# The first block of a fused attention and expert kernel: four head pairs or two halves

## Chip, cores and metric

The kernel runs on one core of a Trainium2 chip. The metric is the time of one execution in microseconds (us), measured on the device. The kernel before takes 502.85 us, the median of 6 runs (502.19 to 503.13).

The engines are named as in the profile: PE is TensorE (matmuls), PEld its weight loads, DVE is VectorE, ACT is ScalarE, POOL is GpSimd, SP is SyncE.

## What is computed

The inputs q, k and v have 8 batches, 8 heads, 1024 positions and 64 dimensions per head. E and F project the 1024 positions of the keys and values to 64. Attention over these 64 projected positions feeds a feed-forward layer with a gated activation.

```python
def _attn_ref(q, k, v, E, F):
    k_proj = np.einsum('ks,bhsd->bhkd', E, k)
    v_proj = np.einsum('ks,bhsd->bhkd', F, v)
    scores = (1.0 / np.sqrt(q.shape[-1])) * np.matmul(q, k_proj.transpose(0, 1, 3, 2))
    scores = scores - np.max(scores, axis=-1, keepdims=True)
    attn = np.exp(scores)
    attn = attn / (np.sum(attn, axis=-1, keepdims=True) + 1e-09)
    return np.matmul(attn, v_proj)

def _moe_ref(x, w_in, w_out):          # x: 8192 x 512, w_in: 512 x 2048, w_out: 2048 x 512
    h = x @ w_in
    g = h * np.clip(h + 3.0, 0.0, 6.0) / 6.0
    return g @ w_out
```

## The kernel before, in words

**Stages.** Every batch of 1024 tokens is worked on as two blocks of 512. For each block the feed-forward layer forms `g` in 16 groups of 128 columns (`fo`), each group from four matmul pairs over `ko` (`first_group`, `h_part`; the matmul itself is line 169, in `in_columns`), and then four groups of output rows (`second_group`). Attention for the next batch is slipped in between these groups at places that the program writes out by hand. The order on each engine is the order in which the Python code issues instructions (`manual_schedule`), so the position of a call in the code is its position in the engine's queue.

**Batch 0.** It has nothing to hide behind. The class `First` handles it, and `first_block` does attention for its first 512 tokens. The heads go in four pairs, `j` = 0 to 3. For each pair:

- `keys(j)` (line 375) projects k by E in 8 matmuls of 128 columns; two DVE copies (line 378) bring the result to `kp`, once for each half of the partitions.
- `queries(0, (j,))` (line 405) transposes q in 4 PE transposes; a DVE copy (line 409) brings it to SBUF.
- `keys_transposed(j)` (line 384) transposes the two heads of `kp`; a DVE copy (line 386) makes `kT`.
- `scores(j)` (line 418) forms the scores in 4 matmuls of 64x64 weights on the four quarters of the array; two exponentials on ACT follow (line 445).
- `sums(j)` (line 425 with `ones` as weights) sums the exponentials on PE; ACT takes the inverse by a logarithm and an exponential (lines 450 and 451).
- `vals(j)` (line 391) projects v by F in 8 matmuls of 128 columns; a copy (line 394) makes `vp`.
- `products(j)` (line 425 with `vp` as weights, then a multiply on DVE, line 454) writes `xT`, the input of the feed-forward layer.

The pairs overlap: `keys` of pair j is issued ahead of `scores` of pair j-1 and `sums` of pair j-2. `meanwhile` puts the first matmul pair of the feed-forward layer (group 0, `ko` 0) into the end of the block. After `first_block` come `ko` 1 and 2 of group 0, `ko` 0, 1, 2 of group 1, `ko` 3 of both, and then the groups from `fo` = 2 on without a break.

**Dummies.** `busy(n)` (line 89) issues n matmuls of 128x512 whose result nobody reads. Twelve of them stand first in PE's queue; their weights are `ones`, which DVE fills at the very start. `ident` is the identity for the PE transposes. POOL makes it (`make_identity`) after its first two DMA issues. E and F are cast by DVE and ACT (lines 140 and 141), transposed by 8 PE transposes (line 145), and copied to `e_t` (line 147, DVE) and `f_t` (line 149, ACT).

**Loads.** POOL issues all loads of q, k, v, `w_in` and `w_out`, which convert to bf16 on the way. For batch 0 the order is k and q by pairs, then v by pairs, then `w_in` in eight pieces, q's second half, `w_out`. Eight semaphores take turns on these DMAs, so each issue waits until the eighth one before it has landed.

**PSUM.** Two pools of four buffers each rotate: `pmm()` (tag mm) and `pat()` (tag at). A tile that is taken waits for the readers of the tile that had its buffer before.

**Batch 1.** `turn` (line 212) turns the projected keys by a transposing DMA on SP; `q_transposed` (line 157) does the same for q in two DMAs, heads 0 to 3 (pairs 0 and 1) and heads 4 to 7 (pairs 2 and 3). `Attention.visit(0)` then issues the scores of three pairs (line 229) with their exponentials (line 238):

```python
js = 2, 0, 1
tiles = [self.scores(j, *two) for j, two in zip(js, ((pmm, pmm), (pat, pat), (pat, pat)))]
```

`visit(1)` starts with the sums and values of pair 0 and the scores of pair 3; `visit(2)` with the sums and values of pair 1.

Of the kernel before, what the change touches and what calls it, by code (L numbers as in the profile page):

```python
# [9 lines left out]
bf16 = mybir.dt.bfloat16  # L10
# [5 lines left out]
def kernel(  # L16
# [11 lines left out]
    nc = tc.nc  # L28
    B, H, S, D = q.shape
    KP = E.shape[0]  # L30
# [3 lines left out]
    P = 128  # L34
    SO = S // P
    KO = d_model // P
    FO = d_ff // P
    TOK = 512
# [42 lines left out]
    ones = consts.tile([P, TOK], bf16, name="ones")  # L81
    nc.vector.memset(ones, 1.0)  # L82
    ident = consts.tile([P, P], bf16, name="ident")


    def busy(n):
        ps = pmm()
        for _ in range(n):
            nc.tensor.matmul(ps, ones[:, :P], ones, start=True, stop=True)  # L89

    busy(12)

    def raw_tile(name):
        return kqv_pool.tile([P, H, SO, D], bf16, tag=name, name=name)


    kqv = {0: {n: raw_tile(n) for n in ("k", "q", "v")}}
    q0 = kqv[0]["q"].rearrange("p h s d -> p (h s d)").rearrange(
        "p (t h s d) -> p t h s d", t=NB, h=H, s=SB)

    def load_q0(t, hs):
        nc.gpsimd.dma_start(out=q0[:, t, hs], in_=kqv_dram["q"][0][:, hs, t * SB:(t + 1) * SB, :])  # L102

    def load_pair(n, j):
        hs = slice(2 * j, 2 * j + 2)
        nc.gpsimd.dma_start(out=kqv[0][n][:, hs], in_=kqv_dram[n][0][:, hs])  # L106

    for j in range(KO):
        load_pair("k", j)
        load_q0(0, slice(2 * j, 2 * j + 2))  # L110
        if j == 0:
            make_identity(nc, ident)
    for j in range(KO):
        load_pair("v", j)

    def load_kqv(b, order="qkv"):
        kqv[b] = {}
# [19 lines left out]
    e_t = consts.tile([P, SO, KP], bf16, name="e_t")  # L137
    f_t = consts.tile([P, SO, 2, KP], bf16, name="f_t")
# [48 lines left out]
    class Attention:  # L187
# [143 lines left out]

        def visit(self, n):
            if n == 0:
                js = 2, 0, 1
                tiles = [self.scores(j, *two) for j, two in zip(js, ((pmm, pmm), (pat, pat), (pat, pat)))]
                for j, two in zip(js, tiles):
                    self.exps(j, two)
                return lambda: None
            if n == 1:
                den, av = self.sums(0, pmm, pmm), self.values(0, pat, pat)  # L340
                last = self.scores(3, pat, pat)
                rec = rec_tile()
# [21 lines left out]
    class First:  # L364
# [4 lines left out]
            self.vp = att.tile([P, H, D], bf16, tag="vp", name="vp")  # L369
            self.qT, self.aT = {}, {}  # L370

        def keys(self, j):
            ps = pat()[:KP, :P]
            for so in range(SO):
                nc.tensor.matmul(ps, e_t[:, so, :], kqv[0]["k"][:, 2 * j:2 * j + 2, so, :],
                                 start=(so == 0), stop=(so == SO - 1))
            for a in range(2):
                nc.vector.tensor_copy(self.kp[:, 2 * j:2 * j + 2, a, :],
                                      ps.rearrange("p (h d) -> p h d", d=D))

        def keys_transposed(self, j):
            ps = pat().bitcast(bf16)[:, :P]
            for a in range(2):
                nc.tensor.transpose(ps[:, a * KP:(a + 1) * KP],
                                    self.kp[:, 2 * j + a].rearrange("p a d -> p (a d)"), ident[:KP, :KP])
            nc.vector.tensor_copy(self.kT[:, 2 * j:2 * j + 2, :].rearrange("p h m -> p (h m)"), ps)

        def vals(self, j, copy):
            ps = pat()[:, :P]
            for so in range(SO):  # L390
                nc.tensor.matmul(ps, f_t[:, so].rearrange("p a m -> p (a m)"),
                                 kqv[0]["v"][:, 2 * j:2 * j + 2, so, :],
                                 start=(so == 0), stop=(so == SO - 1))
            copy(self.vp[:, 2 * j:2 * j + 2, :].rearrange("p h d -> p (h d)"), ps)

        def queries(self, t, js):

            ps = pat().bitcast(bf16)[:, :len(js) * TOK]
            for i, j in enumerate(js):
                for a in range(2):  # L400
                    for m in range(2):
                        o = i * TOK + a * HT + m * P
                        n = width if t else P
                        for lo in range(0, P, n):
                            nc.tensor.transpose(ps[lo:lo + n, o:o + P],  # L405
                                                q0[:, t, 2 * j + a, 2 * m:2 * m + 2, :].rearrange(
                                                    "p s d -> p (s d)")[:, lo:lo + n], ident)
            q = rec_tile().rearrange("p i n -> p (i n)").bitcast(bf16)[:, :2 * TOK]
            nc.vector.tensor_copy(q[:, :len(js) * TOK], ps)
# [24 lines left out]
            return self.quads(lambda r, h: self.vp[r:r + KP, h, :], t, j, alloc)  # L434


        def first_block(self, meanwhile):
            recs = {}

            def scores(j):  # L440
                aT = att.tile([P, 2, HT], bf16, tag="aT0", name="aT0", bufs=KO)
                tiles = [pmm() for _ in range(2)]
                self.scores(0, j, tiles, 0)
                for r in range(2):
                    nc.scalar.activation(aT[:, r], tiles[r][:, :HT], AF.Exp, scale=scale)
                self.aT[0, j] = aT

            def sums(j):
                recs[j] = opool.tile([P, TOK], f32, tag="o_sb", name="o_sb")
                nc.scalar.activation(recs[j], self.sums(0, j, pmm), AF.Ln)  # L450
                nc.scalar.activation(recs[j], recs[j], AF.Exp, scale=-1.0)

            def products(j):
                nc.vector.tensor_mul(self.xT[:, j, 0, :], self.values(0, j, pat), recs[j])

            for j in range(KO):
                self.keys(j)
                if j > 1:
                    sums(j - 2)
                self.queries(0, (j,))  # L460
                if j > 0:
                    scores(j - 1)
                else:
                    busy(1)
                self.keys_transposed(j)
                if j < 2:
                    busy(1)
            scores(KO - 1)
            self.vals(0, nc.vector.tensor_copy)
            sums(KO - 2)  # L470
            self.vals(1, nc.vector.tensor_copy)
            products(0)
            sums(KO - 1)
            self.vals(2, nc.vector.tensor_copy)
            products(1)
            busy(1)
            products(2)
            self.vals(3, nc.scalar.copy)
            meanwhile()
            products(3)  # L480

# [102 lines left out]
    def meanwhile():  # L584
        early.append(TwoGroups(xT, 0, g[0]))
        early[0].part(0, (0,))
# [48 lines left out]
    for b in range(1, B):  # L635
# [36 lines left out]
        for t in range(NB):  # L672
            g = g_tile()
            for fo in range(FO):
# [13 lines left out]
                n = t * SB + slots.index(fo)  # L688
# [43 lines left out]
```

## Time and profile before

| | before |
|---|---|
| median of 6 runs | 502.85 us (502.19 to 503.13) |
| the profiled execution | 502.73 us |
| its span (first to last instruction) | 500.9 us |
| PE busy | 494.2 us (99% of the span) |
| DVE busy | 285.3 us (57%) |
| ACT busy | 239.5 us (48%) |
| POOL busy | 38.6 us (8%) |

In the views, times count from the start of the span. In a row of the timeline the two figures are start and length, then engine, line, operation, tiles (written from read), shape and count; what stands in brackets is how long the engine was idle before and what ended that. A length of several instructions runs from the first start to the last end, and a matmul's end is modelled, so consecutive matmuls overlap in these rows. A busy share near 100% of PE does not mean that PE runs at its full rate.

### The profile page before, as it was taken

Reading aid. Unit: us, or ns where it says so; the run is one execution under the profiler, and the core shown is the slowest. Engines: PE = TensorE matmul, PEld = TensorE weight load, DVE = VectorE, ACT = ScalarE, POOL = GpSimd, SP = SyncE. Lnnn points to the kernel's source line nnn. Section 1 sums busy time; section 2 is a strip of 40 time slices with the busy share of each in tenths; the row PEclk is TensorE's granted clock in tenths of the full one; section 3 lists DMA queues with packets and bytes.
Section 4 is the critical chain, followed back from the end, with each engine's and each line's share of the span. In section 5 each row is a group of like instructions: output and inputs, shape, how many; then the busy total and the mean of one; then the engine's idle time right before and its main releaser. Section 6 shows DMA issues by size and latency. Waiting matters only on the chain.

```text
span 500.9 us, 11177 instructions
## 1 busy us (share of the span) xinstructions
PE 494.2 (99%) x4802; PEld 256.3 (51%) x4802; DVE 285.3 (57%) x438; ACT 239.5 (48%) x414; POOL 38.6 (8%) x58
## 2 busy tenths in 40 slices
PE   8899999999999999999999999999999999999997
PEld 4454544555555545555555555555455555555554
DVE  3581835976659675666648655674755656334420
ACT  3656566665355345433564344643456344343431
POOL 8620020200020020002000020000000000000000
PEclk9999999999999999999999999999999999999999
DMA  9999999897759699549950799309411261101112
GB/s 165 198 204 208 186 175 232 151 208 171 184 95 223 158 205 215 111 117 226 210 114 22 176 192 222 78 24 232 116 43 44 56 180 44 43 22 43 44 43 84
DMA packets 83618, 68.43 MB, mean 137 GB/s; under 512 B 38256, under 2 KB 69232, under 8 KB 83568
## 3 DMA queue, kind: packets, MB, share of 16 engines
q0 software_dynamic: 32480, 29.36, 37.5%
q1 hardware_dynamic: 50864, 38.02, 30.5%
q8 instruction: 37, 0.61, 0.5%
q10 hardware_dynamic: 224, 0.33, 0.3%
q14 instruction: 13, 0.11, 0.1%
HBM read 71.83 MB, written 16.97 MB: 177 GB/s over the span
## 4 chain that ended last, share of the span: by engine, by line
PE 92%; DMA 5%; POOL 2%; SPq 1%; issue 0%; ACT 0%; DVE 0%; ACTq 0%; POOLq 0%
PE mm L169 85%; DMA qT<-q 3%; PE at L169 2%; DMA v<-in_v_dram 2%; PE mm L250 1%; PE at L229 1%; PE at L250 1%; PE mm L229 1%; POOL q L102 1%; POOL k L106 1%; POOL v L106 0%; SPq L157 0%; SPq L212 0%; PE at L425 0%; PE at L405 0%
## 5 line engine op out<-in xcount | busy, mean ns | idle before, releaser
L514 DVE SCALAR_TENSOR_TENSOR g<-r,mm 128x512 bf16<-128x512 f32 x256 | 174.3, 687 | 143.6 <-ACT r L513 142.9
L169 PE MATMUL mm<-w_out_sb,g 128*64 128x512 bf16 (+2 forms) x2080 | 235.6, 376 | 0.0
L169 PE MATMUL mm<-xT,w_in_sb 128*64 128x512 bf16 x2048 | 231.1, 379 | 0.0
L513 ACT ACTIVATE r<-mm 128x512 f32<-128x512 f32 x256 | 152.7, 598 | 74.3 <-PE mm L169 73.3
L169 PEld LDWEIGHTS <-w_in_sb 128*64 128x64 bf16 x2048 | 115.8, 110 | 104.7 <-issue 0.6
L169 PEld LDWEIGHTS <-g 128*64 128x64 bf16 x2080 | 115.0, 110 | 106.3 <-issue 7.1
L548 ACT COPY o_sb<-mm 128x512 f32<-128x512 f32 x58 | 33.9, 585 | 149.8 <-PE mm L169 149.4
L270 DVE TRANSPOSE_TENSOR_REDUCE parts<-aT 128x32 f32<-128x1024 bf16 x24 | 28.8, 1226 | 0.0
L262 DVE TENSOR_TENSOR xT<-at,rec 128x512 bf16<-128x512 f32 x32 | 20.5, 683 | 8.5 <-ACT rec L181 5.8
L238 ACT ACTIVATE aT<-at 128x512 bf16<-128x512 f32 x38 | 20.7, 622 | 8.0 <-PE at L229 8.0
L262 DVE TENSOR_TENSOR xT<-mm,rec 128x512 bf16<-128x512 f32 x24 | 15.5, 686 | 7.3 <-PE mm L250 7.2
L219 POOL COPY mark<-qT 1x1 bf16<-1x1 bf16 x5 | 0.9, 177 | 202.7 <-DMA qT<-q 202.7
L205 DVE CAST kp<-at 64x512 bf16<-64x512 f32 x14 | 9.0, 678 | 11.3 <-PE at L169 11.2
L238 ACT ACTIVATE aT<-mm 128x512 bf16<-128x512 f32 x18 | 9.7, 605 | 7.5 <-PE mm L229 7.5
L169 PE MATMUL at<-k,e_t 128*64 128x512 bf16 x56 | 13.2, 379 | 0.0
L169 PE MATMUL at<-v,f_t 128*64 128x512 bf16 x56 | 13.2, 379 | 0.0
L208 DVE CAST vp<-at 64x512 bf16<-64x512 f32 x14 | 9.7, 694 | 0.4
L538 DVE COPY o_sb<-mm 128x384 f32<-128x384 f32 x1 | 0.6, 558 | 15.2 <-PE mm L169 15.2
L169 PEld LDWEIGHTS <-e_t 128*64 128x64 bf16 x56 | 6.2, 110 | 5.7
L89 PE MATMUL mm<-ones 128*128 128x512 bf16 x18 | 7.3, 540 | 1.5 <-DVE ones L82 1.5
L229 PEld LDWEIGHTS <-kT 64*64 64x64 bf16 x224 | 5.7, 106 | 5.2 <-issue 4.3
L503 DVE TENSOR_TENSOR xT<-at,rec 128x512 bf16<-128x512 f32 x4 | 2.5, 684 | 8.1 <-PE at L425 8.1
(68 smaller groups left out, 151.3 us busy)
## 6 DMA issues: line engine op xcount, KB each, us to landing
out_dram<-o_sb SPq DMA_DIRECT2D x63, 256.0 KB, 4.1
rec<-turned_rows SPq DMA_DIRECT2D x48, 256.0 KB, 6.0
k<-in_k_dram POOLq DMA_DIRECT2D x7, 1024.0 KB, 10.8
v<-in_v_dram POOLq DMA_DIRECT2D x7, 1024.0 KB, 16.0
q<-in_q_dram POOLq DMA_DIRECT2D x7, 1024.0 KB, 20.4
w_out_sb<-in_moe_w_out_dram POOLq DMA_DIRECT2D x4, 512.0 KB, 16.0
w_in_sb<-in_moe_w_in_dram POOLq DMA_DIRECT2D x5, 256.0 KB, 9.8
k<-in_k_dram POOLq DMA_DIRECT2D x4, 256.0 KB, 5.8
```

Source lines behind the costliest of these rows:

```text
L89: nc.tensor.matmul(ps, ones[:, :P], ones, start=True, stop=True)
L169: nc.tensor.matmul(ps[lo:lo + width], stationary[:, lo:lo + width], moving, **flags)
L205: nc.vector.tensor_copy(self.kp[:, :, a, :], self.ps[:KP].rearrange("p (h d) -> p h d", d=D))
L208: nc.vector.tensor_copy(self.vp[a * KP:(a + 1) * KP], self.ps[KP:].rearrange("p (h d) -> p h d", d=D))
L229: nc.tensor.matmul(tiles[r][t * KP:(t + 1) * KP, a * HT:(a + 1) * HT], self.kT[r * D:(r + 1) * D, 2 * j + a, :], qT[r * D:(r + 1) * D, j, ...
L238: when(lambda r=r: nc.scalar.activation(aT[:, :, r, :], tiles[r].rearrange("p (a n) -> p a n", a=2), AF.Exp, scale=scale))
L250: nc.tensor.matmul(tiles[t][c:c + D], stationary(r, 2 * j + a), self.weights(j, a)[r:r + KP], start=True, stop=True)
L262: when(lambda t=t: nc.vector.tensor_mul(self.xT[:, j, t, :], av[t], rec[:, t]))
L270: nc.vector.tensor_reduce(out=self.parts[:, j], op=ALU.add, axis=mybir.AxisListType.X, apply_transpose=True, in_=self.aT[j].rearrange("p a ...
L513: nc.scalar.activation(r, h_ps, AF.Relu, bias=0.5, scale=1.0 / 6.0)
L514: nc.vector.scalar_tensor_tensor(g[:, fo, :], r, 1.0, h_ps, op0=ALU.min, op1=ALU.mult)
L548: (copy or nc.scalar.copy)(o_sb, o_ps)
```

## The change

Batch 0's first block handles the heads in two halves of two pairs instead of four pairs.

- The loads of k and of q's first block come in two pieces each, those of v in three (pairs 0 and 1 together, then 2, then 3).
- `keys` projects a half in 8 matmuls of 256 columns, with two DVE copies of 64x256; `keys_transposed` does four heads and one copy of 128x256; `vals` does pairs 0 and 1 together in matmuls of 256 columns, and pairs 2 and 3 singly, with ACT copying both of these.
- The copies of queries of odd pairs go from DVE to ACT.
- Within a half, all steps of both pairs follow one another: keys, queries, transposes, scores, sums. The sums of pair 3 move into the middle of the first `vals`. `products(2)` moves behind both single `vals`.
- The dummies use `ident` as weights, so they wait for POOL to make it. The first group has 7 of them in place of 12; the block itself has others, at new places.
- Batch 1 issues its scores in the order 0, 1, 2, with the PSUM pools by position as before.

On PE there are 25 matmuls fewer: 16 of `keys`, 8 of `vals` and one dummy.

```diff
     def busy(n):
         ps = pmm()
         for _ in range(n):
-            nc.tensor.matmul(ps, ones[:, :P], ones, start=True, stop=True)
-
-    busy(12)
+            nc.tensor.matmul(ps, ident, ones, start=True, stop=True)
...
-    for j in range(KO):
-        load_pair("k", j)
-        load_q0(0, slice(2 * j, 2 * j + 2))
-        if j == 0:
+    pairs = range(KO)
+    half = KO // 2
+    for js in (pairs[:half], pairs[half:]):
+        load_pairs("k", js)
+        load_q0(0, heads(js))
+        if js[0] == 0:
             make_identity(nc, ident)
-    for j in range(KO):
-        load_pair("v", j)
+            busy(7)
+    for js in (pairs[:half], *([j] for j in pairs[half:])):
+        load_pairs("v", js)
...
             if n == 0:
-                js = 2, 0, 1
+                js = 0, 1, 2
...
-        def vals(self, j, copy):
-            ps = pat()[:, :P]
+        def vals(self, js, copy, halfway=lambda: None):
+            ps = pat()[:, :len(js) * P]
             for so in range(SO):
-                nc.tensor.matmul(ps, f_t[:, so].rearrange("p a m -> p (a m)"),
-                                 kqv[0]["v"][:, 2 * j:2 * j + 2, so, :],
+                nc.tensor.matmul(ps, f_t[:, so].rearrange("p a m -> p (a m)"), kqv[0]["v"][:, heads(js), so, :],
                                  start=(so == 0), stop=(so == SO - 1))
-            copy(self.vp[:, 2 * j:2 * j + 2, :].rearrange("p h d -> p (h d)"), ps)
-
-        def queries(self, t, js):
+                if so == SO // 2 - 1:
+                    halfway()
+            copy(self.vp[:, heads(js), :].rearrange("p h d -> p (h d)"), ps)
+
+        def queries(self, t, js, copy=nc.vector.tensor_copy):
...
-            for j in range(KO):
-                self.keys(j)
-                if j > 1:
-                    sums(j - 2)
-                self.queries(0, (j,))
-                if j > 0:
-                    scores(j - 1)
-                else:
-                    busy(1)
-                self.keys_transposed(j)
-                if j < 2:
-                    busy(1)
-            scores(KO - 1)
-            self.vals(0, nc.vector.tensor_copy)
-            sums(KO - 2)
-            self.vals(1, nc.vector.tensor_copy)
+            for js in (pairs[:half], pairs[half:]):
+                self.keys(js)
+                if js[0] == 0:
+                    busy(2)
+                for j in js:
+                    self.queries(0, (j,), nc.scalar.copy if j % 2 else nc.vector.tensor_copy)
+                self.keys_transposed(js)
+                busy(1)
+                for j in js:
+                    scores(j)
+                busy(2)
+                for j in js[:None if js[0] == 0 else -1]:
+                    sums(j)
+            self.vals(pairs[:half], nc.vector.tensor_copy, lambda: sums(KO - 1))
             products(0)
-            sums(KO - 1)
-            self.vals(2, nc.vector.tensor_copy)
             products(1)
-            busy(1)
+            self.vals((2,), nc.scalar.copy)
+            self.vals((3,), nc.scalar.copy)
             products(2)
-            self.vals(3, nc.scalar.copy)
             meanwhile()
             products(3)
```

More of the change, by code (lines that the diff above doesn't have):

```diff
@@ L99, with heads, load_pairs @@
         "p (t h s d) -> p t h s d", t=NB, h=H, s=SB)
+    def heads(js):
+        return slice(2 * js[0], 2 * js[-1] + 2)
     def load_q0(t, hs):
         nc.gpsimd.dma_start(out=q0[:, t, hs], in_=kqv_dram["q"][0][:, hs, t * SB:(t + 1) * SB, :])
-    def load_pair(n, j):
-        hs = slice(2 * j, 2 * j + 2)
+    def load_pairs(n, js):
+        hs = heads(js)
         nc.gpsimd.dma_start(out=kqv[0][n][:, hs], in_=kqv_dram[n][0][:, hs])
-    for j in range(KO):
-        load_pair("k", j)
-        load_q0(0, slice(2 * j, 2 * j + 2))
-        if j == 0:
+    pairs = range(KO)
[4 more added lines that the diff above has]
+        if js[0] == 0:
             make_identity(nc, ident)
-    for j in range(KO):
-        load_pair("v", j)
+            busy(7)
+    for js in (pairs[:half], *([j] for j in pairs[half:])):
+        load_pairs("v", js)
     def load_kqv(b, order="qkv"):
@@ L370, in __init__, with keys @@
             self.qT, self.aT = {}, {}
-        def keys(self, j):
-            ps = pat()[:KP, :P]
+        def keys(self, js):
+            ps = pat()[:KP, :len(js) * P]
             for so in range(SO):
-                nc.tensor.matmul(ps, e_t[:, so, :], kqv[0]["k"][:, 2 * j:2 * j + 2, so, :],
+                nc.tensor.matmul(ps, e_t[:, so, :], kqv[0]["k"][:, heads(js), so, :],
                                  start=(so == 0), stop=(so == SO - 1))
             for a in range(2):
-                nc.vector.tensor_copy(self.kp[:, 2 * j:2 * j + 2, a, :],
-                                      ps.rearrange("p (h d) -> p h d", d=D))
@@ L381, in keys_transposed @@
[L381 to L386, printed above, removed]
-        def vals(self, j, copy):
-            ps = pat()[:, :P]
+                nc.vector.tensor_copy(self.kp[:, heads(js), a, :], ps.rearrange("p (h d) -> p h d", d=D))
@@ new lines, in keys_transposed @@
+        def keys_transposed(self, js):
+            ps = pat().bitcast(bf16)[:, :len(js) * P]
+            for i in range(2 * len(js)):
+                nc.tensor.transpose(ps[:, i * KP:(i + 1) * KP],
+                                    self.kp[:, 2 * js[0] + i].rearrange("p a d -> p (a d)"), ident[:KP, :KP])
+            nc.vector.tensor_copy(self.kT[:, heads(js), :].rearrange("p h m -> p (h m)"), ps)
+        def vals(self, js, copy, halfway=lambda: None):
+            ps = pat()[:, :len(js) * P]
@@ L408, in queries @@
             q = rec_tile().rearrange("p i n -> p (i n)").bitcast(bf16)[:, :2 * TOK]
-            nc.vector.tensor_copy(q[:, :len(js) * TOK], ps)
+            copy(q[:, :len(js) * TOK], ps)
             for i, j in enumerate(js):
```

## Prediction

> **What bounds the kernel now.** I read the page first: its span and the busy line.
>
> ```profile
> span 500.9 us, 11177 instructions
> ...
> PE 494.2 (99%) x4802; PEld 256.3 (51%) x4802; DVE 285.3 (57%) x438; ACT 239.5 (48%) x414; POOL 38.6 (8%) x58
> ```
>
> TensorE (PE) is busy for all but 6.7 us, and no other engine for more than 57%. A change ahead of the steady stream is therefore worth what it moves the stream's start. The chain of waits for the first 36 us tells what sets that start:
>
> ```profile
> 9.79 9.75 DMA v<-in_v_dram
> ...
> 19.59 0.62 PE at L391 x8
> 20.21 0.34 PE mm L169 x2
> ...
> 20.57 0.40 PE at L425 x2
> 20.97 12.86 PE mm L169 x118
> ```
>
> Columns are start, length, what. The last quarter of v is issued at 9.79 and lands at 19.54; eight projections, a product and then 118 matmuls follow with no gap. The timeline of PE gives durations, and a second hole at batch 1's scores:
>
> ```profile
> 1.46 5.13 PE L89 MATMUL mm<-ones 128*128 128x512 bf16 x12 [1.46 <-DVE ones L82]
> ...
> 6.94 0.59 PE L89 MATMUL mm<-ones 128*128 128x512 bf16 x2
> 7.62 0.63 PE L375 MATMUL at<-k,e_t 128*64 128x128 bf16 x8
> ...
> 20.90 12.93 PE L169 MATMUL mm<-xT,w_in_sb 128*64 128x512 bf16 x118
> ...
> 66.96 1.89 PE L169 MATMUL mm<-w_out_sb,g 128*64 128x512 bf16 x16
> 69.16 0.41 PE L229 MATMUL mm<-qT,kT 64*64 64x256 bf16 x8 [0.31 <-DMA qT<-q]
> ```
>
> Twelve dummies take 5.13 us, 0.43 each; two later ones start 0.22 apart. So PE runs at half rate at first and at full rate from about 6.3, 4.8 us after its first matmul, though the granted-clock column says 1.00 in all these rows. Next, DMA by stretch (the last figure is GB/s, the third from the end the granted clock):
>
> ```profile
> 5.50:7.50 2.00, 2.00 (x13) 0.92 (x11) 0.63 (x2) 0.45 (x1) 2.00 (x3) 1.00 1.17 143
> 9.50:17.50 8.00, 7.10 (x87) 4.46 (x85) 3.81 (x14) 5.57 (x14) 5.49 (x8) 1.00 1.28 204
> ```
>
> Last, of POOL's timeline, the row that finishes `ident`:
>
> ```profile
> 3.07 0.29 POOL masks.py:199 TENSOR_SCALAR_AFFINE_SELECT ident<-ident 128x128 bf16<-128x128 bf16 x1
> ```
>
> As yardstick I take the start of column group fo=2. Before it come seven pairs from 20.90: 0.24 + 6 x 0.2155, so 22.44.
>
> **Loads.** Twelve issues of k, q, v become seven, bytes unchanged. POOL saves 5 x 0.72 us of issuing, on no path: POOL then waits for landings. The stretch 5.5 to 7.5 moved 143 GB/s against 204 later; a queue filled with larger pieces could win back 2 x 61/204 = 0.6 us. So v's last quarter lands between 18.9 and, if nothing improves, 19.54. I take 19.0; either serves, as the next part shows. Later loads (w_in and on) move with it and have slack.
>
> **The first block's chain.** What the halves do to PE's order matters more. Four short rounds, each filling the others' waits, become two long ones, in which PE stands behind its own copies. On the clock of the trace:
>
> Start. `ident` is ready at 3.36 now; two larger issues ahead of it (0.77 us for a 512 KB one against 0.72) make it 3.45. The dummies, and all that PE has queued behind them, now wait for it and start at 3.5 instead of 1.46. What hides this wait: the first real work, E and F, is cast only at 5.96. Seven dummies at 0.427 reach 6.5. If full rate comes 4.8 us after the start, as now, it comes at 8.3; then the eight transposes cost a quarter of a dummy, 0.107 each (0.06 now), their last ends at 7.55, and e_t is copied by 8.0 (0.42). The two dummies behind run until 8.3. First keys: 8.3, against 7.62.
>
> First half. Keys, 8 x 256 columns: 8 x 0.109 (half of 0.216) and the last one's way out, 1.05: 9.35. Two kp copies, 64x256, do not occur now; 64x128 takes 0.28 (starts 0.20 apart), 64x512 0.68 (0.60 apart). On the line between, 0.42 and 0.33 apart: done by 10.17. Two dummies (0.53) and eight query transposes (0.056 each and change-overs) hold PE until 10.37. Key transposes 0.30 (0.23 for two now), kT copy 128x256 0.34 with its wait (between 0.22 and 0.42): 11.0. Scores 0.30 and a wait: 11.36. Four exponentials, 3 x 0.263 + 0.38: 12.56. The two dummies ahead of the sums take scores 0's first PSUM buffer (four rotate), so they start only at 11.8, after its first exponential; sums 0 and 1 end at 13.0. Leg: 4.7 us.
>
> Second half. Its keys stand behind sums(1) in PE's queue, so nothing of it starts before 13.0, though all of k lands sooner (its last quarter releases an issue of POOL at 13.00 already now). The same terms bring the scores to 15.6, their exponentials to 17.1; sums(2), half of the vals and sums(3) end at 18.0. The copy of query 3, now on ACT (0.585), stands behind sum 1's two activations and ends at 15.72, just under scores(2); without that cover it would cost its overhang, up to 0.5. Leg: 5.0.
>
> Values. The rest of vals (0.44 and drain) to 18.6, the vp copy 128x256 (0.29 to 0.69; taken 0.42) to 19.1, products 0 and 1 on different quadrants together 0.34 (products(0) and sums(3) at 17.04 and 17.05 do that now), vals 2 and 3 at 0.55 each: 20.57. v's last quarter is wanted at 20.0, so its landing is hidden by 0.5 us or more. Then products(2) 0.33, the first h matmuls 0.24, products(3) 0.33: 21.47. Pair ko=1 0.24; ko=2 waits for products(2)'s multiply (21.0 + 0.69), 0.05; five more pairs and it is 23.04. Against 22.44: **+0.6 us**. The stall for v is gone; the chain of copies is late instead. Ends of the unknown copies: two kp pairs, 0.75 taken of 0.48 to 1.28; two kT, 0.29 of 0.22 to 0.42; one vp, 0.42 of 0.29 to 0.69. Together -0.8 to +1.6. I take the line between rows, since each new size lies between two measured ones.
>
> **Batch 1's order.** Scores of pair 2 need the second of two transposing DMAs of q, pairs 0 and 1 the first. SP issues them at 61.23 and 63.24; they land 6.1 and 5.8 us later: 67.3 and 69.03. PE is free at 66.96 + 8 x 0.2155 = 68.68 and starts at 69.16. With pair 0 first nothing is awaited, and pair 2's turn comes 2 x 0.216 later, at 69.13, past the landing. Gain **0.45 us**. SP's issues follow the kp copy, so the hole moves along with PE. The exponentials keep their count; the first sums want pair 0, now done first; buffers come free in the old order. Nothing new waits.
>
> **Sum.** +0.60 - 0.45 = +0.15 us. The profiled execution took 502.73 us (span 500.9 and 1.8 around it), 0.12 under the median, so it goes to 502.9 and the median, 502.85, to **503.0**.
>
> The Trainium skill (TensorE: Matmul & The Clock Gate, Part 1) speaks against starting PE later: full rate wants a busy window of about 3.4 us that runs free, so a start at 3.5 may meet its first whole window anywhere from 6.9 to 10.3. The row shows 4.8 us after the start, once. By the page, as an estimate, the sum would lie between -0.35 and +1.2.
>
> The same skill's DMA: Bandwidth & Descriptors (Anatomy of one DMA) puts some 2 us of fixed time on each transfer, which as an estimate would give 5 x 2 = 10 us for five fewer. The stretch at 204 GB/s with several in flight shows that this time is overlapped here.
>
> **Rivals.** *Late full rate (slower).* If PE stays at half rate until the key transposes of the first half, 10.4 in my chain, its eight keys cost 0.107 us more each, 0.85, and the query transposes ahead of the key transposes some 0.2: 0.6 + 1.05 = +1.65 at fo=2, +1.2 in all, **504.1**. Half rate through that whole half, to 13, is the far end: scores, sums and dummies at twice their time as well, some 1.1 more, +2.8 and 505.2. It decides past +1.0, that is from a full rate later than about 9.9. For it: the start is 2 us later, and the time to full rate is a single reading. Against it: dummies are dense from 3.5 to 8.3.
>
> *The landing bounds it (faster).* POOL's issues that v's landings release stand at 14.96, 16.23, 17.52 and 19.83: the last quarter took 2.3 us, the others 1.3. Without that 1.0 and the 0.6 of the dip v lands at 18.0. If the halves also overlap better than I count, fo=2 could start 2.9 us later as now, and 0.2 for products(2) now behind that landing: 21.1, so -1.3 - 0.45, **501.1**. Against it: at full rate from the first matmul on the same chain still gives 22.2.
>
> *The order does nothing.* If both transposes land together, the 0.45 stays: **503.45**. The landings 67.3 and 69.03 speak against it.
>
> **How the numbers follow.** 0.2% is 1.0 us, about what a measurement of this kernel can tell from no change: 501.85 to 503.86. My forecast (from full rate at 6.3, -0.5, to full rate at 9.5, +0.8) 0.58, no effect of the order 0.05: within, 0.63. Late full rate 0.27: slower. Landing 0.10: faster. The range 501.9 to 504.4 takes in the copies' ends but for the topmost 0.2, and leaves out the landing case and the upper third of the late one, about 0.2.
>
> **What would show it.** Right: L89 dummies from 3.5, still 0.43 apart; first keys near 8.3; second keys near 13; PE waiting for DVE and ACT in this block and not for v at its end; fo=2 near 23.0; no DMA wait ahead of batch 1's scores. Wrong: matmuls at half rate after 9.9, a wait for v at the end, fo=2 before 22.4, or a hole that stays near 69.

## The result and the profile after

The kernel after takes 504.29 us, the median of 20 runs (503.37 to 506.64), against 502.85 us of 41 runs of before (502.17 to 503.82). The ratio is 1.003, 95% interval 1.0023 to 1.0037: slower by 0.3%, or 1.44 us. That lies inside the predicted range (501.9 to 504.4), but 1.3 us above the forecast of 503.0, and beyond the bound of 503.86 from which "slower" was counted.

The profiled execution of after took 504.08 us, 1.35 more than that of before. The page's span and busy line, and the group of output matmuls:

```profile
span 502.3 us, 11113 instructions
...
PE 493.0 (98%) x4776; PEld 257.5 (51%) x4777; DVE 283.5 (56%) x428; ACT 240.9 (48%) x417; POOL 35.2 (7%) x53
...
L173 PE MATMUL mm<-w_out_sb,g 128*64 128x512 bf16 (+2 forms) x2080 | 235.7, 376 | 0.9 <-DVE g L515 0.9
```

The same group in before's page:

```profile
L169 PE MATMUL mm<-w_out_sb,g 128*64 128x512 bf16 (+2 forms) x2080 | 235.6, 376 | 0.0
```

PE's busy time went down by 1.2 us and the span up by 1.4. The output matmuls, with 0.0 of idle time in before, have 0.9 us of it now; that wait lies far from the edited block. The timeline of PE, first block and batch 1's scores:

```profile
3.52 3.17 PE L89 MATMUL mm<-ones,ident 128*128 128x512 bf16 x7 [3.52 <-POOL ident masks.py:199]
...
8.32 1.36 PE L379 MATMUL at<-k,e_t 128*64 128x256 bf16 x8
...
12.05 0.38 PE L89 MATMUL mm<-ones,ident 128*128 128x512 bf16 x1 [0.37 <-ACT aT L450]
...
13.21 1.06 PE L379 MATMUL at<-k,e_t 128*64 128x256 bf16 x8
...
15.11 0.29 PE L387 MATMUL at<-ident,kp 64*128 64x64 bf16 x4 [0.29 <-DVE kp L382]
...
19.43 0.41 PE L429 MATMUL at<-aT,vp 64*64 64x512 bf16 x4 [0.52 <-DVE vp L398]
...
67.87 1.89 PE L173 MATMUL mm<-w_out_sb,g 128*64 128x512 bf16 x16
69.69 0.41 PE L233 MATMUL mm<-qT,kT 64*64 64x256 bf16 x8
```

The brackets name DVE and ACT as what PE waits for, and no load. The first keys take 1.36 us and the second 1.06 with the same shapes: the first ran partly at half rate (the trace's clock records have full rate from 8.96 us; 6.30 in before). Column group fo=2 starts at 23.32, 0.88 later than in before. At 69.69 the hole ahead of the scores is closed, and PE stands 0.53 behind before, 0.35 less than at fo=2. From the chain of waits near 126 us (start, length, what):

```profile
114.63 3.27 DMA turned_rows<-inv
...
120.46 5.58 DMA rec<-turned_rows
...
126.16 1.29 DVE xT L266 x2
127.45 0.60 DVE g L515
...
128.10 1.05 PE mm L173 x8
```

The timelines of DVE and of PE there:

```profile
126.16 1.29 DVE L266 TENSOR_TENSOR xT<-at,rec 128x512 bf16<-128x512 f32 x2 [1.65 <-DMA rec<-turned_rows]
```

```profile
128.10 1.05 PE L173 MATMUL mm<-w_out_sb,g 128*64 128x512 bf16 x8 [0.89 <-DVE g L515]
```

Batch 2's inverse softmax sums go out to DRAM (`turned_rows`) and come back spread over partitions (`rec`). DVE stands waiting for the second pair's `rec`, the next `g` waits behind that in DVE's queue, and PE waits for `g`. The same matmuls start at 126.51 in before, so PE's delay against before goes from 0.53 to 1.59 us here; by 184 us some 0.2 of it is regained. First block +0.88, the closed hole -0.35, return of the sums +1.06, later -0.2: the 1.35 us of this execution, to within 0.05.

Before was already close to this. Its PE does not wait there, and only DVE's timeline shows it (PE's row first):

```profile
126.51 1.03 PE L169 MATMUL mm<-w_out_sb,g 128*64 128x512 bf16 x8
```

```profile
122.25 1.29 DVE L262 TENSOR_TENSOR xT<-at,rec 128x512 bf16<-128x512 f32 x2 [1.79 <-DMA rec<-turned_rows]
124.41 1.29 DVE L262 TENSOR_TENSOR xT<-at,rec 128x512 bf16<-128x512 f32 x2 [0.87 <-DMA rec<-turned_rows]
```

### The profile page after: what moved, and what is told of

It reads as the page before. It is cut to its first block, busy times and chain, and to the rows that moved or that the text cites. A ratio compares the mean times of both kernels' runs of the same rounds, so it can differ in the third digit from the quotient of the medians.

```text
span 502.3 us, 11113 instructions
## 1 busy us (share of the span) xinstructions
PE 493.0 (98%) x4776; PEld 257.5 (51%) x4777; DVE 283.5 (56%) x428; ACT 240.9 (48%) x417; POOL 35.2 (7%) x53
## 4 chain that ended last, share of the span: by engine, by line
PE 94%; DVE 2%; DMA 2%; SPq 1%; ACT 0%; issue 0%; POOL 0%; DVEq 0%; ACTq 0%; POOLq 0%
PE mm L173 85%; PE at L173 2%; DMA rec<-turned_rows 1%; PE mm L254 1%; PE mm L89 1%; PE at L233 1%; DMA turned_rows<-inv 1%; PE at L254 1%; PE mm L233 1%; SPq L297 0%; PE at L429 0%; PE at L379 0%; PE at L394 0%; DVE kp L382 0%; PE mm L429 0%
## 5 line engine op out<-in xcount | busy, mean ns | idle before, releaser
L173 PEld LDWEIGHTS <-w_in_sb 128*64 128x64 bf16 x2048 | 117.4, 110 | 103.3 <-issue 0.9
L89 PE MATMUL mm<-ones,ident 128*128 128x512 bf16 x16 | 6.6, 522 | 4.2 <-POOL ident masks.py:199 3.5
```

The source lines that it names most:

```text
L89: nc.tensor.matmul(ps, ident, ones, start=True, stop=True)
L173: nc.tensor.matmul(ps[lo:lo + width], stationary[:, lo:lo + width], moving, **flags)
```

## Experiments

Every time is the median of 4 to 12 executions; what stands in brackets behind it is the lowest and highest, and a ratio is to before's executions beside them, with its 95% interval. "Offset" is how much later an instruction of PE starts than the same one in before's profile; a "step" is a change of the offset, and the one near 126 us is always the return of batch 2's sums. Landings and clock changes are read from the trace's own records. Only one execution of each version was traced, and it can be an untypical one: 502.37 us for `order_only` against a median of 503.38, 505.49 for `early_dummies` against 503.97.

**The order alone, the halves alone.** `order_only` is before with the new order, `halves_only` is after with the old one.

```diff
-js = 2, 0, 1
+js = 0, 1, 2      # order_only, on before; the reverse in halves_only, on after
```

> The kernel before with batch 1's scores in the order 0, 1, 2, and nothing else. Theory A (three terms: the first block +0.9 us, the order -0.35 to -0.45, and a wait for batch 2's sums to come back from DRAM, +0.9, that the later first block and the later loads of batch 3 open): the hole ahead of batch 1's scores closes, PE is 0.4 us early from there on, the wait near 126 us stays closed: 502.4. Rival B (the order itself shifts the loads of batches 2 and 3 and so opens the wait near 126 us): the 0.4 is won and 0.9 lost, 503.3, with PE idle on DVE's g near 126 us.

> The changed kernel with batch 1's scores back in the order 2, 0, 1: the halves, loads and dummies alone. Theory A: fo=2 starts 0.6 to 1.6 us later than before (by the moment of full rate), no gain at batch 1, and the wait near 126 us is open or not by how late the loads of batch 3 are: 504.0 to 504.9. Rival B (the order opens the wait): 503.7 with no wait there.

`order_only`: 503.38 us (502.07 to 504.32), ratio 1.0003 (0.9993 to 1.0013). `halves_only`: 504.03 us (503.31 to 507.31), ratio 1.0025 (1.0011 to 1.0039). The slowdown belongs to the halves. In `order_only` the order does close the hole (offset -0.56 behind the scores, -0.18 ahead of them), but at 126 us the offset is back at -0.14. Its PE timeline there:

```profile
126.37 1.05 PE L169 MATMUL mm<-w_out_sb,g 128*64 128x512 bf16 x8 [0.25 <-DVE g L514]
```

A gain ahead of this place is clipped by the return of the sums: `rec` lands at 124.31 here as at 124.29 in before. The time is that of rival B, but not for its reason, since nothing came later than in before. In `halves_only` the offset falls from +0.45 ahead of the scores to +0.08 behind them, though the order is the old one: its first transposing load of q takes 4.5 us instead of 6.1, and the hole closes without the new order. After's own offset falls by as much there, from +0.91 to +0.53. So nothing shows that the order gains anything in after. In `halves_only` the offset then steps to +0.81 near 126 us.

**Batch 3's k and v held back.** Those loads, 2 MB, run from 97 to 117 us, and the sums' way out and back begins at 114. They are held here until batch 2's `rec` has landed, in after and in before:

```diff
-load_kqv(self.b + 1, "qkv" if self.b == 2 else "kvq")
+load_kqv(self.b + 1, "q" if self.b == 2 else "kvq")
...
+nc.gpsimd.tensor_copy(mark, second.recs[KO - 1][:1, 0, :1])
+load_kqv(3, "kv")
```

> The changed kernel with batch 3's loads of k and v held back until batch 2's inverse sums have come back from DRAM; q's load stays. Theory A: the eight transfers of inverse sums have the DMA engines to themselves and land a microsecond or more sooner, PE does not wait near 126 us: 503.4, and the slowest runs go most. Rival C (the wait in the one profile is an accident, and the typical excess comes from a first block that reaches full rate later than in that profile): unchanged, 504.1 to 504.4.

> The kernel before with the same two loads held back. Its profile shows no wait near 126 us. Theory A: 502.6 to 502.9, the transfers land sooner but nothing waited for them, at most the upper runs lose some tenths. Rival D (the held loads open a wait of their own at batch 3's projection): slower by 0.5 or more, which would spoil the reading of the same edit on the changed kernel.

513.14 and 512.97 us: the hold opens a wait of its own. PE's timeline in `kv_late_after`:

```profile
137.86 0.38 PE L173 MATMUL at<-k,e_t 128*64 128x512 bf16 x1 [1.86 <-DMA k<-in_k_dram]
144.87 0.58 PE L173 MATMUL at<-v,f_t 128*64 128x512 bf16 x1 [6.63 <-DMA v<-in_v_dram]
```

These times settle nothing about the slowdown, but the traces do say something of the return: `turned_rows` lands 1.5 us after its issue in both, instead of 2.9 (before) and 3.3 (after), and there is no step near 126 us.

**Moving PE's instruction fetches.** The DMA engines also bring PE its instructions, 16 KB at a time (queue q8). With 25 matmuls fewer the fetches of after fall elsewhere: one now lies in batch 2's first transposing load of q, which took 5.24 us instead of 4.45, and batch 3's loads start behind that load. The views of DMA during batch 1's first such load show the same thing from the other side, for before (61 to 67.4 us) and after (62 to 66.7). Columns are queue and kind, packets, MB, and the time that they took as a share of 16 engines over the stretch:

```profile
q1 hardware_dynamic: 3394, 0.85, 105.7%
q8 instruction: 1, 0.02, 0.9%
```

```profile
q1 hardware_dynamic: 3286, 0.83, 95.8%
```

Before has one instruction packet beside the transposes there, and its load takes 6.1 us; after has none, and 4.5.

I added small matmuls in the idle time at the start to move the fetches (in `after_pad72` each dummy is cut in four as well), and put after's dummies back to twelve on `ones` in one more kernel:

```diff
+    def pad(n):
+        ps = pmm()
+        for _ in range(n):
+            nc.tensor.matmul(ps[:32, :64], ones[:, :32], ones[:, :64], start=True, stop=True)
+
+    pad(25)        # after_pad25; pad(21) in after_pad72; pad(53), busy(7) for busy(12) in order_pad48
```

```diff
-        for _ in range(n):                                     # after_pad72, busy
-            nc.tensor.matmul(ps, ident, ones, start=True, stop=True)
+        for _ in range(4 * n):
+            nc.tensor.matmul(ps[:, :P], ident, ones[:, :P], start=True, stop=True)
```

```diff
-            nc.tensor.matmul(ps, ident, ones, start=True, stop=True)   # early_dummies, busy
+            nc.tensor.matmul(ps, ones[:, :P], ones, start=True, stop=True)
+    busy(12)
...
-            busy(7)
```

> After, with 25 matmuls of 32x64 on ones put ahead of the ident dummies, so that TensorE's stream has as many instructions ahead of batch 1 as in before and its 16 KB instruction fetches fall where they fell in before. Theory F (fetches): after issues 25 matmuls fewer, its fetch moved from 89 us to 93.7 us, into batch 2's first transposing load of the queries (5.24 us instead of 4.45), so batch 3's loads start later, meet turned_rows and rec, and the inverse sums return 1 us later than the offset alone would have it. With the fetch back at 89 to 90 us that load takes 4.4 to 4.5 us again, the offset at 126 to 128 us is at most +0.8 instead of +1.59, and the time is about 503.6. Batch 1's first load is hit instead (6.1 us instead of 4.5), behind which the scores in the order 0, 1, 2 leave a small hole. Rival O (offset alone): batch 3's loads are late because TensorE is 0.5 us late, the load's length being incidental: the wait near 126 us stays, and the time is 504.2. The early matmuls may also bring the full rate sooner (before 8.96 us), which shows in the offset of the first block and is kept apart from the step at 126 us.

> After, with 21 matmuls of 32x64 on ones ahead of the ident dummies and each 512-column dummy cut into four of 128 columns: 72 instructions pairs more than after, 47 more than before. By theory F the fetches fall some 5 us earlier than in before, about 60 and 84 us, so that neither batch 1's nor batch 2's transposing loads of the queries holds one: 4.5 and 4.4 us both. The offset behind batch 1's scores is then as in after or lower, the step at 126 us is under 0.3, and the time is 503.2 to 503.6, less than with 25. Rival O: the step at 126 us stays at 1 us whatever the loads take, and the time is 504.2.

> Before with batch 1's pairs in the order 0, 1, 2, and five of the twelve dummies replaced by 53 of 32x64: 48 matmuls more than before, the first block else as in before. By theory F the fetches move 5 us earlier, batch 1's first load of the queries takes 4.5 us instead of 6.1, so that the hole ahead of batch 1's scores closes (offset -0.5 behind them), and the loads of batch 2 and 3 start as early as TensorE allows; the return of the inverse sums, which took the gain back in the run with the order alone, comes 0.3 to 0.6 us sooner. Time 502.4 to 502.8 against 502.9 to 503.2 of before. Rival O: the return near 126 us stays where it is in before, and the time is that of before.

> After, with the dummies of before: twelve on ones from 1.5 us on, and the later ones on ones, instead of seven on ident from 3.5 us on. It tests the term of the late start alone. Theory: in after the full rate comes at 8.96 us, in the middle of the first keys, because TensorE's work starts 2 us later; with the early dummies it comes by 5 to 7 us, the first keys take 1.06 instead of 1.36 each, and the offset of the first block falls from +0.87 to +0.3 to +0.5. Rival: the first block is set by the loads and the chain of copies, and the early start gives less than 0.2. The time also moves by what the fetches do (five matmuls more at the start): 503.6 to 504.2 if the step at 126 us stays.

`after_pad25` 504.79 us (ratio 1.0028, 1.0016 to 1.0040), `after_pad72` 504.59 (1.0023, 1.0012 to 1.0033), `order_pad48` 502.56 (0.9994, 0.9986 to 1.0003), `early_dummies` 503.97 (1.0017, 1.0009 to 1.0026). The fetches moved as meant, and the transposing loads followed: with a fetch in it batch 2's first one took 5.1 to 5.3 us (or the kT load ahead of it was held up), without one 4.4. But theory F, that this causes the step, falls, though `order_pad48` took the time that it gave. `after_pad72` has no fetch in either batch's load and issues batch 3's loads at 96.17 (96.10 in before), and yet the step is +0.10 to +1.51. Its chain of waits:

```profile
114.19 3.88 DMA turned_rows<-inv
...
120.10 5.86 DMA rec<-turned_rows
...
128.02 1.05 PE mm L180 x8
```

What does hold in all eight profiles with batch 3's loads in their old place: `turned_rows` lands 0.3 to 0.4 us behind the last piece of batch 3's v, wherever that lands (116.1 to 119.4), and the second pair's `rec` 7.3 to 8.1 us behind `turned_rows`. And wherever `rec` decides, the offset at 126.5 us is its landing less 124.45, to 0.01 us: 124.31 gives -0.14, 125.15 gives +0.70, 126.04 gives +1.59, 127.43 gives +2.98. Before itself (124.29) had only 0.16 us to spare.

`early_dummies` took a time within its expectation, but not for the reason given there. Full rate came at 5.04 us, and yet the first block of its traced execution, the slowest of twelve, was the latest of these four (offset +1.69, expected +0.3 to +0.5). Its PE timeline names why:

```profile
9.45 1.03 PE L380 MATMUL at<-k,e_t 128*64 128x256 bf16 x8 [1.58 <-DMA k<-in_k_dram]
```

The first half of k had landed at 9.41. Whether the late start costs something in the other executions is open: the ratio is below after's 1.0030 (1.0023 to 1.0037), but the intervals overlap.

**Only v held back,** until the second pair's `rec` has landed, in before, in after and in the padded version of the order:

```diff
+load_kqv(self.b + 1, "qk" if self.b == 2 else "kvq")
...
+nc.gpsimd.tensor_copy(mark, second.recs[1][D:D + 1, 0, :1])
+load_kqv(3, "v")
```

> Before, with only batch 3's load of v held until the second pair's inverse sums of batch 2 have landed (q and k stay where they are). In eight profiles turned_rows lands 0.3 to 0.4 us behind the end of that load, and the pair's last rec 7.3 to 8.1 us behind turned_rows. Theory R (return): with the load out of the way turned_rows lands 1.3 to 1.8 us sooner, the pair's rec at about 123 instead of 124.3, TensorE was bound there by 0.1 us at most, so that before gains nothing that can be measured: 502.5 to 503.2. Issued at about 123.5, v lands at 130 to 133 by the 8.6 us that k took in the run with both loads held, ahead of its need at 135.9. Rival: the held load opens a wait of its own at 135.9, and the time is 504 or more.

> The same hold in after. Theory R: nearly all of the 1.4 us by which after is slower comes of the step of +1.06 us near 126 us, where products of batch 2 await the inverse sums; with rec landing about 1.3 us sooner the step is gone, the offset stays at that of the first block less the gain of the order (0 to +0.5), and the time is 503.0 to 503.5. Rival P: the step is only where an offset of TensorE becomes visible, some other work (the longer first block, VectorE) carries the 1.4 us, and the time stays at 504.2. Rival: a wait for v at 137.

> The same hold in the version with the pairs in the order 0, 1, 2 and the 48 small matmuls (502.56 without the hold). Theory R: that version came to 126 us with an offset of -0.73 and was held there by rec to -0.50; with rec sooner it keeps -0.7, a gain of 0.2 to 0.3: 502.2 to 502.5, below both kernels. Rival: v is awaited at 135, and the time is 503 or more.

| | median, us | lowest to highest | ratio to before (95%) |
|---|---|---|---|
| before, beside them | 503.01 | 502.08 to 503.91 | |
| `v_late_before` | 502.37 | 501.98 to 502.94 | 0.9986 (0.9978 to 0.9995) |
| `v_late_after` | 503.69 | 502.44 to 505.44 | 1.0014 (1.0001 to 1.0028) |
| `v_late_order_pad` | 501.83 | 501.55 to 504.30 | 0.9980 (0.9970 to 0.9990) |

v lands at 134 to 137 us and is not awaited. All three times lie outside what theory R gave: before gains 0.64 us, where nothing was expected, and its profile, with no wait of PE, had not shown that; `v_late_order_pad` gains more than expected, and after less. In after the gain is not clear of noise: the ratio is 1.0014 where after had 1.0030 (1.0023 to 1.0037), and the intervals overlap.

In after the hold also did only half of what it was for. `turned_rows` lands 1.5 us after its issue in all three versions. Behind it the second pair's `rec` takes 7.6 us in `v_late_before` and in `v_late_order_pad`, but 9.0 in `v_late_after`. So `rec` lands at 123.20 in `v_late_before`, 1.1 sooner than in before, and at 125.79 in `v_late_after`, 0.25 sooner than in after, where `turned_rows` is issued 0.7 sooner. DVE's timeline in `v_late_after`:

```profile
125.91 1.29 DVE L266 TENSOR_TENSOR xT<-at,rec 128x512 bf16<-128x512 f32 x2 [2.31 <-DMA rec<-turned_rows]
```

The rule from above holds here too: 125.79 less 124.45 is +1.34, and that is the offset at 126.5 us (+1.19 ahead of it). `rec` still decides there, so that this run does not tell what after would take with the return out of the way. Between the landings of the second and the third `rec` 2.5 us pass, against 1.1 in `v_late_before`, and a fetch of PE's instructions, begun at 121.20, runs into that stretch; in `v_late_before` it begins at 115.47. That the fetch causes it is not shown: in `kv_late_after` one begins at 119.14, and `rec` takes 7.8 us behind `turned_rows`. Padding and hold together, in after, would test it and were not run.

Where the two held versions differ in their traces can be told: `v_late_after` is +1.55 at fo=2 and regains 0.38 at the hole, the step at 126 us adds 0.15, and at the end it is 1.3 us later than `v_late_before`. In the medians the two are 1.32 us apart. The lowest and highest lie 3.0 us apart in `v_late_after` and 1.0 in `v_late_before`. The profiled execution of `v_late_after` shows the same wait as that of `early_dummies`, on PE's timeline:

```profile
9.31 1.03 PE L379 MATMUL at<-k,e_t 128*64 128x256 bf16 x8 [0.92 <-DMA k<-in_k_dram]
```

The clock adds to the spread as well. The two slowest executions of `v_late_after` (505.44 us both) have a mean granted clock of 0.997, and so have the slowest of after (506.64) and of `halves_only` (507.31); of the 29 executions of before beside them one has it (503.11). In the traced execution of `v_late_order_pad` a mean of 0.993 stands for 6.83 us at half rate; by that row 0.997 would be some 3 us, an estimate.

**The first half of k as two loads,** on top of `v_late_after`, with the matmuls as wide as before:

```diff
-        load_pairs("k", js)
-        load_q0(0, heads(js))
+        for part in ([[j] for j in js] if js[0] == 0 else [js]):
+            load_pairs("k", part)
         if js[0] == 0:
             make_identity(nc, ident)
             busy(7)
+        load_q0(0, heads(js))
```

> The version of after with v held, and in addition the first half of k loaded as its two pairs (two DMAs, both ahead of ident's making and of the queries' load) instead of one DMA of twice the size; the keys' matmuls stay wide. Theory K (the landing of k): in seven profiles with the load by halves the first keys start 0.05 us behind the load's last piece, which lands at 8.06 to 9.41, and the offset of the first block is that landing less 7.6 to 7.65 (0.44 to 1.76, but 0.87 to 0.96 in after's own profile, where half rate adds to it); in the kernels of before the first pair lands at 6.06 to 6.70 and nothing waits for it. With two loads the second should land at 7.2 to 7.6, the keys start where the dummies end (8.1 to 8.4) in every execution, the offset of the first block is 0.45 to 0.75, the time 502.6 to 503.0 and its spread (lowest to highest) about 1 us instead of 3. Rival C (clock): the late full rate of after, not the landing, carries the first block, so that median (503.7) and spread stay.

503.37 us (502.41 to 504.23), ratio 1.0005 (0.9994 to 1.0015), not clear of the 1.0014 (1.0001 to 1.0028) of `v_late_after`; the spread is 1.8 us instead of 3.0. I expected the second pair at 7.2 to 7.6 us; it landed at 8.58 and was awaited again:

```profile
8.72 1.03 PE L380 MATMUL at<-k,e_t 128*64 128x256 bf16 x8 [0.61 <-DMA k<-in_k_dram]
```

So in this trace the smaller size of the load does not bring its last piece sooner: the first pair lands at 6.51, the second at 8.58. In the six profiles with single pairs the second pair lands at 8.28 to 8.79, and nothing waits for it, because the first keys want the first pair alone. That wanting two pairs is what costs was not tested by a version with narrow keys and the rest of after. The return decides here as well: `rec` lands at 125.64, 9.4 us behind `turned_rows` (again with an instruction fetch in between, at 120.75), and the offset steps from +0.60 to +1.19:

```profile
127.70 1.05 PE L174 MATMUL mm<-w_out_sb,g 128*64 128x512 bf16 x8 [0.42 <-DVE g L516]
```

The eight profiles with the halves, against four of the six with single pairs (us; "fo=2" and "126.5" are offsets there):

| | last piece of k wanted by the first keys | first keys | fo=2 | 126.5 |
|---|---|---|---|---|
| before | 6.06 | 7.62 | 0 | 0 |
| `order_only` | 6.28 | 7.40 | -0.18 | -0.14 |
| `order_pad48` | 6.28 | 7.77 | -0.35 | -0.66 |
| `v_late_before` | 6.34 | 7.50 | +0.01 | +0.02 |
| `kv_late_after` | 8.06 | 8.12 | +0.37 | +0.02 |
| `after_pad25` | 8.09 | 8.13 | +0.36 | +0.70 |
| `after_pad72` | 8.14 | 8.19 | +0.45 | +1.51 |
| `halves_only` | 8.15 | 8.20 | +0.42 | +0.81 |
| after | 8.27 | 8.32 | +0.88 | +1.59 |
| `v_late_split_k` | 8.58 | 8.72 | +0.95 | +1.19 |
| `v_late_after` | 9.27 | 9.31 | +1.55 | +1.34 |
| `early_dummies` | 9.41 | 9.45 | +1.69 | +2.98 |

In all eight with the halves the keys start 0.04 to 0.14 us behind the landing, and in six of them PE's timeline names k as what it waited for. In after and `kv_late_after` the dummies ended at about the same moment. But for after, where half rate adds some 0.3, the offset at fo=2 is the landing less 7.63 to 7.73. The six profiles with single pairs have 0.8 to 1.6 us to spare between the first pair's landing and the first keys (6.06 to 7.62 in before), so that a late piece of that load is absorbed. With the halves each late piece went into the start of fo=2. Where the landing is latest, it is one engine's share that is: in `v_late_after` the first of the 16 DMA engines ends at 7.07, as in after (7.08), fifteen are done by 8.00, and the last ends at 9.27.

**Not settled.** Each version was traced in a single execution; that k's landing varies as much over the untraced ones would fit the spreads and was not seen. How the 1.44 us between the medians divide into k's landing, the return of the sums and the clock is therefore open. Why one engine is late in some executions is open as well, and so is why batch 3's loads took 20.1 us in after and 21.5 in `after_pad72`.

## Why the prediction was off

**What held.** Dummies from 3.52 (predicted 3.5), first keys at 8.32 (8.3), second keys at 13.21 (13.0), waits for DVE and ACT in the block, no wait for v at its end, and the hole ahead of batch 1's scores closed. v's last quarter landed at 18.64 (19.0). The sum of the legs held too: from the first keys to fo=2 it gives 14.74 us, and `kv_late_after`, whose keys run at full rate, has 14.69. That 504.29 lies in the stated range is luck: its upper part was there for late copies and a late full rate, and what filled it, the return of the sums, was in no term.

**Mis-sized terms.** The first block is +0.88 instead of +0.60: full rate came at 8.96 us where 8.3 was taken, so the first keys took 1.36 us instead of 1.05. The range from the clock (-0.5 to +0.8) holds this. *Late full rate*, whose point was 9.9, did not occur in after's trace. The moment scatters: it came 2.8 (`halves_only`), 4.3 (`kv_late_after`), 4.35 (`v_late_split_k`) and 5.4 us (after, `v_late_after`) behind the first dummy on `ident`, and before's 4.8 was one reading. By the Trainium skill (TensorE: Matmul & The Clock Gate, Part 1), which wants a busy window of about 3.4 us, it would, as an estimate from a start at 3.52, be at 6.9 us or later; 6.28 in `halves_only` is sooner than that, and the measurement decides. The hole gave 0.38 instead of 0.45. And the order is not shown to have closed it in after: in `halves_only` it closes by as much in the old order, since no instruction fetch falls into the transposing load there. That this sign came true is luck.

**The step that failed in the traced execution:** that a change ahead of the steady stream is worth what it moves the stream's start, and, at batch 1, that nothing new waits. The stream has a second bound near 126 us, the return of batch 2's sums. In after's profiled execution it gave +1.06 us, the largest term. Reading "PE 99%" and 0.0 of idle time for line 169, I did not ask how much was to spare: DVE's own waits for `rec`, 1.79 and 0.87 us, were in before's trace. The same bound took back what `order_only` had gained.

**The step that failed in other executions: "First keys: 8.3".** It was worked out from dummies, E and F and the clock alone. That the first keys now want 512 KB of k, which land at 8.06 at the earliest seen, stood in no term; the part on loads followed only v's last quarter. Before's trace held a warning: there the second quarter of k lands at 8.79. In after's own trace landing (8.27) and dummies ended together, so that the step came out right by luck. In three of the seven others the landing was 0.3 to 1.1 us later, and the whole chain behind it moved along. The step should have been the later of two times, and the one that scatters should have widened the range upwards.

Which of the two weighs more in the medians is not shown. Holding v was meant to take the return out, and in both held versions of after `rec` still decided at 126 us.

**The rivals.** *The landing bounds it* looked at v's landing and on the faster side; in several traces it was k's, and on the slower one. *The order does nothing* is wrong for the hole in `order_only`, and right in effect for its median; in after the hole closes with either order.

The experiments lead to a version below both kernels: pairs in the order 0, 1, 2, small matmuls for five of the dummies, batch 3's v held. `v_late_order_pad` takes 501.83 us, 0.2% less than before.

## What to carry over

When steps are merged to fill waits, ask what the first merged step now needs from memory, and when its last piece lands: a smaller step's slack against a late DMA engine is worth keeping, and a profile of a good execution does not show what it is worth. A busy share of 99% does not say that the stream can be moved: look through the other engines' waits for a place where a DMA returns just in time, for it can clip a gain and add to a delay. When a wait is to be taken out for a test, look in the trace whether it is gone before the time is read. Trace several executions before a term of under 1 us is put down to one cause.

## What was unexpected of the hardware

- A fetch of PE's instructions in the midst of a transposing load lengthens it: batch 1's first load of q takes 6.1 to 6.2 us with one (five profiles) and 4.5 without (nine), batch 2's 5.1 to 5.3 against 4.4, apart from `early_dummies`, where the fetch stretched the kT load ahead of it from 2.6 to 4.4 us. So some dozens of instructions more or fewer at the start change how long a DMA takes 50 us further on.
- A small transfer through DRAM, `turned_rows`, ends 0.3 to 0.4 us behind the 1 MB load that is under way when it is issued (eight profiles), though another engine issued that: it takes 2.9 to 3.9 us (4.3 in `early_dummies`), and 1.5 where the load is held back (six).
- PE can fall back to half rate. In the profiled execution of `v_late_order_pad` (504.30 us; its eleven others 501.55 to 502.12) PE waited 0.53 us for q, and the clock records show half rate from 15.41 to 22.24 us. In both versions with k and v held it falls too, from 141 to 148 us, during the wait of 6.6 us for v. Eight projections of v took 1.04 us in `v_late_order_pad` and 0.62 in before:

```profile
14.63 0.40 PE L412 MATMUL at<-ident,q 128*128 128x128 bf16 x4 [0.53 <-DMA q<-in_q_dram]
...
16.10 1.04 PE L398 MATMUL at<-v,f_t 128*128 128x128 bf16 x8
```
